# One core, a recurrent attention with a two-layer MLP behind it: the u row on ScalarE's DMA queue, and a new order of all operations

## The chip, the cores and the metric

The kernel runs on one core of a Trainium2 chip. A core has five engines with an instruction stream each: TensorE (PE in the profile; its weight loads are listed apart as PEld), VectorE (DVE), ScalarE (ACT), GpSimd (POOL) and SyncE (SP). Each of them takes its instructions in program order, and waits on semaphores that the others raise. DMA transfers are issued by an engine's instruction stream and run beside the engines.

The metric is the device time of one launch in microseconds, less is better. The kernel before takes 183.4 us, the median of three runs (182.93 to 184.22). "Within 1%" below means within 1.8 us.

## The reference, cut to what matters

Batch B = 4, heads H = 8, sequence S = 768, head dimension D = 48; the attention's output is the MLP's input, with 3072 tokens, 384 channels and 2048 hidden units.

```python
for t in range(S):
    cur = np.einsum('bhd,bhe->bhde', u[None] * kt, vt)
    y[:, :, t] = np.einsum('bhd,bhde->bhe', rt, state + cur)
    state = wt[:, :, :, None] * state + np.einsum('bhd,bhe->bhde', kt, vt)
...
h = x @ w_in
r = np.maximum(h, 0.0)
g = s * (r * r) + b
return (g @ w_out).astype(np.float32)
```

`u` is one row of 8 x 48 numbers. It enters only through `sum_d r*k*u` of the same step, a scalar for each token and head, which multiplies v.

## The kernel before, in words

The sequence is cut into 24 chunks of 128 tokens (6 for each of 4 batches), numbered n = 0 to 23. Two chunks make one tile T of 256 tokens for the MLP, so T = 0 to 11. Chunks 0 to 3 are "packed": two of them are loaded and decayed together (`load2`, L316; `load`, L308, for the others).

The steps of a chunk have short names, which the order uses. `load n.0` to `n.3` fetch w, r, k and v. `ln` takes the logarithm of w on ScalarE, `cum` sums it over the tokens with a triangular matmul (L390, L397, L408), `exp` (L438) and, from chunk 8, `inc` and `exn` give the decays. `mul` (L465, L472, VectorE) multiplies r and k by them, `tr` (L521) transposes the products on TensorE and `tev` copies them out of PSUM; from chunk 9 a transposing DMA replaces both. `mt` (L588, L600) forms the 128 x 128 scores, `msk` (L612, VectorE, four for a pair of chunks) masks them, `ymm` (L637, L650, L659) multiplies them by v (cast by `vb`). `rkp` and `rku` (L344, L350, GpSimd) form r*k and r*k*u, `cd` (L367, VectorE) sums over d, and `yd` (L373, GpSimd) multiplies v by it. `dmm`, `sup` (L759, L767) and `st` (L776) carry the state. `yev` brings the output to SBUF: for a packed chunk by the helper `move`, which takes ScalarE or VectorE as the order says; for the others by one VectorE instruction that also adds `yd` (L741). `xtr` (L787) transposes it, `xev` copies it into the tile's input.

The MLP of a tile is eight steps `g1 T.i` (six matmuls each, L841; step i needs the weight piece that its columns lie in: pieces 0 and 1 for i = 0 and 1, piece 2 for i = 2 and 3, and so on), each followed by `relu T.i` (L854) and `sq T.i` (L864 on ScalarE, L866 on VectorE), and eight steps `g2 T.i` (four matmuls each, L884), with `oev` (L895) and `store` at the end. The weights arrive in five pieces: `li` loads and `ci` casts a piece of w_in, `lo` and `co` one of w_out (L809, L821, casts at L964, L966, L968). `csred`, `csadd`, `cssplit`, `csspread` and `csevac` sum w_out over its rows for the bias b (L925, L932, L935, L943, L949).

The order of all of this is written out by hand as one text, `ORDER`. A program walks it word by word and emits each operation's instructions at once, so each engine's stream is the text's order, cut down to that engine. `name@A`, `@D` or `@P` sets the field `eng` of the operation to ScalarE, VectorE or GpSimd; `+6` puts in six matmuls on zeros (L1263) that keep TensorE occupied. Whether a mark has an effect is up to the operation's function: `move` and `cast` read the field, `square` and `csred` and `csadd` do. Two functions do not, that of `relu` and, for chunks 4 to 23, that of `yev`:

```python
        nc.scalar.activation(out=rh, in_=hs[T, i], func=AF.Relu)
...
        nc.vector.tensor_tensor(
            out=x,
            in0=c["y_ps"][:, 0:HD],
            in1=c["yd"].rearrange("t h d -> t (h d)"),
            op=ALU.add,
        )
```

All DMAs go out from SyncE, in the text's order. `load_u` (L983) is the second of them; `u_mm` (L987) then spreads the row over 128 partitions by a matmul with ones, and `u_ev` copies it to `u_bc`, which `rku` reads. Each DMA takes one of eight completion semaphores in turn, so a DMA can be issued only when the eighth before it has landed.

PSUM has six buffers "P" (cum, tr, mt, ymm, dmm, xtr, g1) and two "o" (g2, and the packed chunks' ymm); a buffer is given on in the text's order.

Of the kernel before, what the change touches and what calls it, by code (L numbers as in the profile page):

```python
# [18 lines left out]
U_AT = 3.5  # L19
# [23 lines left out]
load0.0 load_u load0.1 load0.2 ln0 +6 u_mm cum0.0 cum1.0 cum1.1 exp0.0 exp0.1 load2.0 li0 load2.1  # L43
exp1.0 u_ev@A l20 l21 load0.3 rkp1 rku1 load2.2 mul0.0 mul0.1 +4 tr0 exp1.1 mul1.0 ln2 +4 cum2.0
rkp0 mul1.1 tr1 tev0@D exp2.0 cum3.0 cd1 tev1@A vb0@A exp2.1 vb1@A +3 mt0 rku0 li1 cum3.1 ci0@A rkp3
exp3.0 rkp2 mul2.0 load2.3 msk1.0 exp3.1 ci1@A li3 li2 msk0.0 lo0 msk1.1 +3 ymm0.0 msk0.1 cd0 dmm0
ymm0.1 mul2.1 sup0 yd0 yd1 vb3@A vb2@A rku3 st0 mul3.0 l23 sup1 load4.0 tr2 ymi0 ydm0 lo1 rku2
mul3.1 tr3 tev2@A yev0@A xtr0 yev1@D xtr1 xev0@D ci3@P cd3 tev3@A xev1@A ci2@A mt2 cd2 g10.0 msk2.0
yd2 g10.1 l22 yd3 relu0.0 co0@A li4 msk3.0 msk2.1 co1@P g10.2 ymm2.0 lo2 ln4 lo3 load5.0 dmm2 msk3.1
sup2 ymm2.1 st2 g10.3 csred0@D ydm2 cum4.0 sq0.0@A relu0.2 ci4@P relu0.1 ymi2 yev2@D g10.4 sq0.2@A  # L50
relu0.3 xtr2 sup3 csred1@D exp4.0 sq0.1@D small2 g10.5 co2@D g10.6 xev2@A lo4 yev3@A xtr3 csadd1@D
sq0.3@A relu0.4 csred2@D relu0.6 load4.1 g10.7 relu0.5 g20.4 xev3@A sq0.4@A co3@D ln5 csadd2@D
sq0.5@A g20.0 cum4.1 g20.5 g20.1 g11.0 g11.1 load4.3 load7.0 csred3@D relu0.7 co4@D sq0.6@A csadd3@D
cum5.0 g11.2 sq0.7@A load5.1 load4.2 l24 csred4@D small cum5.1 g20.6 load5.2 relu1.1 relu1.0 g20.2
relu1.2 exp4.1 csadd4@D cssplit sq1.0@A load5.3 g20.3 g11.3 mul4 g11.4 vb5@P exp5.0 g11.5 exp5.1
sq1.1@A sq1.2@A vb4@A relu1.3 relu1.4 rkp4 rkp5 g20.7 csspread g11.6 tr4 load8.0 load6.0 csevac mul5
rku4 l25 oev0.1 relu1.5 tev4@A tr5 tev5@D oev0.0 rku5 dmm4 load7.3 load6.1 sup4 load6.2 relu1.6
g11.7 g21.0 mt4 msk4.0 msk5.0 load6.3 load7.1 sq1.3@A sq1.4@A sq1.5@A sq1.6@A relu1.7 st1 g21.1
g21.4 g21.5 dmm5 ln6 load9.0 msk4.1 cd4 yd4 ymm4 cum6.1 msk5.1 cum6.0 ln7 cd5 sup5 ln8 st4 exp6.0
cum7.0 g21.2 sq1.7@A exp6.1 vb6@A g21.6 cum7.1 yev4 exp7.0 vb7@P st5 ymm5 g21.3 xtr4 exp7.1 cum8.0  # L60
yd5 l26 ln9 mul6 tr6 yev5 xev4@D st3 load7.2 exp8.0 xtr5 dmm6 mul7 cum9.0 g21.7 tr7 tev6@A inc8
xev5@A sup6 load10.0 load11.0 l28 dmm7 load8.3 load8.1 load11.3 load9.1 l27 sup7 exp9.0 g12.0 g12.1
tev7@A relu2.0 inc9 oev1.0 rkp6 mt6 rku6 rkp7 relu2.1 store0.0 load8.2 msk6.0 sq2.1@A g12.2 ln10
sq2.0@A g12.3 st7 cd6 exn9 exn8 relu2.3 relu2.2 sq2.3@A load9.2 store0.1 msk6.1 oev1.1 g12.4 msk7.0
sq2.2@A rku7 st6 yd6 msk7.1 g22.0 ymm6 g22.4 load9.3 g12.5 cd7 yev6 relu2.4 ymm7 g12.6 yd7 vb8@P
xtr6 cum10.0 g12.7 rkp9 l29 mul8 ln11 relu2.5 exp10.0 rkp8 relu2.6 xev6@D load10.1 yev7 g22.1 inc10
# [24 lines left out]
load18.2 store4.1 store4.0 rku17 g16.7 rku16 sq6.3@A sq6.2@A sq6.5@A load20.0 yev15 sq6.4@D load21.1
xtr14 cum19.0 dmm16 g26.0 load21.0 load19.1 xtr15 g26.1 xev14@D relu6.6 g26.2 xev15@D sup16 relu6.7
sq6.7@A exp19.0 g17.0 g17.1 cd17 relu7.0 load20.1 inc19 cd16 sq7.0@A vb17@P yd16 vb18@A load19.2
mt16 msk16.0 msk16.1 g26.5 sq6.6@A g17.2 msk17.0 st16 relu7.1 g26.6 dmm17 sup17 msk17.1 g17.3 ymm16
g26.7 yev16 oev6.1 rkp18 relu7.2 relu7.3 ymm17 g17.4 load20.2 yd17 st17 g26.3 xtr16 oev6.0 sq7.1@A
exn18 xev16@D yev17 g17.5 g17.6 load21.2 load19.3 ln20 exn19 rku18 mul18 g27.4 xtr17 sq7.2@A relu7.4
g27.0 g17.7 sq7.4@A relu7.5 relu7.6 ln21 sq7.5@D store5.0 xev17@D cum20.0 sq7.3@A rkp19 relu7.7 cd18
g18.0 mul19 l219 g18.1 vb19@P rku19 exp20.0 sq7.6@A load22.0 inc20 sq7.7@D cum21.0 g18.2 g27.5 g27.1
g27.6 exn20 relu8.0 tev18 g18.3 relu8.1 relu8.2 exp21.0 g27.2 dmm19 store5.1 sq8.2@A g27.3 g27.7
mul20 inc21 exn21 dmm18 relu8.3 sq8.0@D tev19 sq8.1@A cd19 mul21 g18.4 load23.0 g18.5 yd19 rkp20  # L100
g18.6 sup18 tev21 sup19 oev7.1 oev7.0 relu8.4 ln22 yd18 rkp21 mt18 sq8.3@A relu8.5 g28.0 st18
msk19.0 supn21 msk18.0 msk19.1 tev20 msk18.1 load20.3 rku20 g28.4 g18.7 load22.1 store6.1 relu8.6
# [66 lines left out]
def kernel(  # L169
# [812 lines left out]
    def load_u():  # L982
        nc.sync.dma_start(out=u_row, in_=u.rearrange("h d -> (h d)").unsqueeze(0))  # L983
# [320 lines left out]
```

## Time and profile before

| What | Value | How to read it |
|---|---|---|
| Median of 3 runs | 183.4 us | 182.93 to 184.22 |
| Profiled execution, first to last instruction | 180.1 us | the only time that the page gives for it; 3.3 us less than the median, which lie around the span |
| TensorE clock granted | 1.00 in every stage | no throttling in this run |
| matmuls `g1` (L841) | 576, 72.2 us busy | 0.65 us for a step of six, back to back |
| matmuls `g2` (L884) | 400, 72.3 us busy | 0.65 us for a step of four, back to back |
| zero matmuls (L1263) | 20, 7.2 us busy | all before 15 us |
| relu (L854, ScalarE) | 96, 597 ns each | 54.5 us busy |
| square on ScalarE / VectorE | 77 of 635 ns / 19 of 534 ns | L864, L866 |
| DMA queues | one, 34.22 MB | 82.0% of 16 engines' span |

Busy time is counted once where instructions of an engine overlap in part. Four masks in a row take 2.48 us where one alone takes 0.68.

### The profile page before, as it was taken

How to read it: one execution, taken by the hardware profiler on the slowest of the kernel's cores; microseconds unless marked ns; L12 is line 12 of the kernel's file. 1: busy time of each engine (PE TensorE's matmuls, PEld its weight loads, DVE VectorE, ACT ScalarE, POOL GpSimd, SP SyncE). 2: the span in 40 equal slices, each digit the busy share in tenths (PEclk: the TensorE clock that was granted, in tenths of full speed). 3: DMA queues.
4: the chain of work that ended last, by engine and by line, in shares of the span. 5: the costliest groups of instructions: out<-in, count | busy, mean ns of one | idle time of the engine just before them, and what ended most of it. 6: DMA issues, size and time to landing. Idle time of an engine off the chain costs nothing.

```text
span 180.1 us, 4874 instructions
## 1 busy us (share of the span) xinstructions
PE 172.5 (96%) x1880; PEld 132.4 (74%) x1880; DVE 139.4 (77%) x251; ACT 143.4 (80%) x281; POOL 105.2 (58%) x141
## 2 busy tenths in 40 slices
PE   6997789999999999999999999999999999999993
PEld 2364568787688877888876879688777796796872
DVE  7499879998989899688699789678779795750341
ACT  2668799999999999798989769679968869266850
POOL 3687963009988987990689269484388382620000
PEclk9999999999999999999999999999999999999999
DMA  5999999999898969979988976999949845622022
GB/s 136 319 275 280 384 398 349 233 190 220 173 228 195 194 133 185 206 180 240 189 192 158 241 159 131 226 216 210 192 93 220 195 108 118 186 73 67 0 87 87
DMA packets 115722, 34.53 MB, mean 192 GB/s; under 512 B 110065, under 2 KB 113906, under 8 KB 115698
## 3 DMA queue, kind: packets, MB, share of 16 engines
q1 hardware_dynamic: 115698, 34.22, 82.0%
q8 instruction: 14, 0.23, 0.5%
q14 instruction: 10, 0.08, 0.2%
HBM read 25.17 MB, written 4.72 MB: 166 GB/s over the span
## 4 chain that ended last, share of the span: by engine, by line
PE 85%; SPq 7%; DMA 5%; ACT 1%; issue 0%; DVE 0%
PE o_ps L884 35%; PE h_ps L841 35%; DMA wi_st<-in_moe_w_in_dram 5%; SPq L316 5%; PE mt_ps L600 3%; PE cums L408 2%; PE y_ps L659 2%; SPq L809 2%; PE y_ps L650 2%; PE xt_ps L787 2%; PE d_ps L724 2%; PE trps L521 1%; ACT w_in L964 1%; PE cums L414 1%; PE yp_ps L637 0%
## 5 line engine op out<-in xcount | busy, mean ns | idle before, releaser
L841 PE MATMUL h_ps<-xT,w_in 128*128 128x256 bf16 x576 | 72.2, 273 | 0.6 <-ACT w_in L964 0.6
L884 PE MATMUL o_ps<-w_out,gT 128*128 128x384 bf16 (+2 forms) x400 | 72.3, 320 | 0.0
L854 ACT ACTIVATE rh<-h_ps 128x512 bf16<-128x512 f32 x96 | 54.5, 597 | 17.3 <-PE h_ps L841 16.8
L841 PEld LDWEIGHTS <-w_in 128*128 128x128 bf16 x576 | 60.0, 110 | 6.4 <-ACT w_in L964 0.9
L884 PEld LDWEIGHTS <-gT 128*128 128x128 bf16 x400 | 36.0, 98 | 18.0
L864 ACT ACTIVATE gT<-rh 128x512 bf16<-128x512 bf16 x77 | 47.0, 635 | 0.4
L612 DVE TENSOR_TENSOR mt_sb<-mt_ps,tri_strict 128x512 bf16<-128x512 f32 x40 | 25.5, 684 | 6.0 <-PE mt_ps L600 5.8
L350 POOL TENSOR_TENSOR rku<-rkp,u_bc 128x384 f32<-128x384 f32 x24 | 25.9, 1081 | 0.7 <-DVE cd L367 0.2
L373 POOL TENSOR_TENSOR yd<-vt,cd 128x384 bf16<-128x384 f32 x20 | 17.9, 896 | 13.6 <-DMA vt<-in_v_dram 6.4
L344 POOL TENSOR_TENSOR rkp<-rkt 128x384 f32<-128x384 f32 x20 | 20.1, 1008 | 4.7 <-DMA rkt<-in_k_dram 4.7
L472 DVE TENSOR_TENSOR prd<-rkt,E 128x768 bf16<-128x768 f32 x20 | 21.9, 1101 | 0.2 <-ACT E L438 0.2
L438 ACT ACTIVATE E<-cums 128x388 f32<-128x388 f32 (+2 forms) x32 | 15.3, 495 | 5.5 <-POOL rku L350 1.7
L895 DVE SCALAR_TENSOR_TENSOR o_sb<-o_ps,s_bc,bconst 128x384 f32<-128x384 f32 (+2 forms) x25 | 14.8, 596 | 5.8 <-PE o_ps L884 5.7
L966 POOL CAST vb<-vt 128x384 bf16<-128x384 f32 x11 | 7.5, 679 | 16.4 <-DMA vt<-in_v_dram 16.4
L866 DVE TENSOR_TENSOR gT<-rh 128x512 bf16<-128x512 bf16 x19 | 10.0, 534 | 7.5 <-ACT rh L854 7.5
L776 POOL TENSOR_TENSOR st<-stmp,l 128x384 bf16<-128x384 bf16 x16 | 14.7, 918 | 0.4 <-DVE stmp L767 0.4
L508 POOL TENSOR_TENSOR l<-E,par 128x8 f32<-128x8 f32 x20 | 6.9, 353 | 11.8 <-ACT E L438 11.7
L741 DVE TENSOR_TENSOR x_sb<-y_ps,yd 128x384 bf16<-128x384 f32 x20 | 10.7, 552 | 4.0 <-PE y_ps L659 4.0
L367 DVE TENSOR_REDUCE cd<-rku 128x8 f32<-128x384 f32 x24 | 13.0, 543 | 0.3 <-POOL rku L350 0.3
L767 DVE TENSOR_TENSOR stmp<-d_ps,st 128x384 bf16<-128x384 f32 x16 | 8.6, 551 | 2.2 <-PE d_ps L724 1.7
L465 DVE TENSOR_TENSOR prd<-pkt,E 128x384 bf16<-128x384 f32 x8 | 7.0, 892 | 2.3 <-ACT E L438 2.2
L446 DVE TENSOR_TENSOR inc<-cums,logw_two 128x384 f32<-128x384 f32 x11 | 6.1, 551 | 3.0 <-PE cums L414 1.7
(103 smaller groups left out, 205.4 us busy)
## 6 DMA issues: line engine op xcount, KB each, us to landing
wt<-in_w_dram SPq DMA_DIRECT2D x20, 192.0 KB, 4.0
rkt<-in_r_dram SPq DMA_DIRECT2D x20, 192.0 KB, 3.7
vt<-in_v_dram SPq DMA_DIRECT2D x20, 192.0 KB, 3.5
rkt<-in_k_dram SPq DMA_DIRECT2D x20, 192.0 KB, 3.8
out_dram<-o_sb SPq DMA_DIRECT2D x19, 192.0 KB, 2.8
wi_st<-in_moe_w_in_dram SPq DMA_DIRECT2D x3, 768.0 KB, 8.1
wo_st<-in_moe_w_out_dram SPq DMA_DIRECT2D x3, 768.0 KB, 5.9
pkt<-in_w_dram SPq DMA_DIRECT2D x2, 384.0 KB, 4.4
```

The source lines that it names most:

```text
L344: nc.gpsimd.tensor_tensor(out=rkp, in0=c["r"], in1=c["k"], op=ALU.mult)
L350: nc.gpsimd.tensor_tensor(out=rku.rearrange("t h d -> t (h d)"), in0=c["rkp"].rearrange("t h d -> t (h d)"), in1=u_bc, op=ALU.mult,)
L373: nc.gpsimd.tensor_tensor(out=yd, in0=c["v"], in1=c["cd"].unsqueeze(2).to_broadcast([128, H, D]), op=ALU.mult,)
L438: nc.scalar.activation(out=c["E"][:, x, 0:w], in_=ps[:, 0:w], func=AF.Exp, scale=-1.0 if packed(n) and x else 1.0,)
L472: nc.vector.tensor_tensor(out=prd[:, :, :, 0:D], in0=c["rk"], in1=c["E"][:, :, 0:HD].rearrange("t x (h d) -> t x h d", h=H), op=ALU.mult,)
L612: nc.vector.tensor_tensor(out=c["mt"][:, sg], in0=c["mt_ps"][sg], in1=(masks[:, n % 2] if packed(n) else tri_strict) .unsqueeze(1) .to_bro ...
L776: nc.gpsimd.tensor_tensor(out=c["st_new"], in0=c["stmp"].rearrange("q p (g e) -> q p g e", g=2), in1=c["l2"].unsqueeze(3).to_broadcast([12 ...
L841: nc.tensor.matmul(ps[:, f, :], lhsT=w_in_sb[PIECE[ft]][:, kt, :].rearrange("p (m j) -> p j m", j=PIECES[PIECE[ft]])[:, ft - F0[PIECE[ft]] ...
L854: nc.scalar.activation(out=rh, in_=hs[T, i], func=AF.Relu)
L864: nc.scalar.activation(out=g, in_=rh, func=AF.Square)
L884: nc.tensor.matmul(os_[T, k][:, cols], lhsT=gT[T][:, ft, tt * 128 : (tt + 1) * 128], rhs=w_out_sb[PIECE[ft]][:, ft - F0[PIECE[ft]], cols], ...
L895: nc.vector.scalar_tensor_tensor(out=o_sb[:, cols], in0=os_.pop((T, k))[:, cols], scalar=s_bc, in1=bconst[:, cols], op0=ALU.mult, op1=ALU.add,
```

## The change

The row u is loaded by a DMA that ScalarE issues as its first instruction, ahead of the load of its activation table; `load_u` is gone from SyncE's stream and from the plan. The order text is new from beginning to end. The numbers of zero matmuls go from 6, 4, 4, 3, 3 to 4, 2, 2, 2, 4, at other places. Nothing else in the code differs.

```diff
-U_AT = 3.5
...
 ORDER = """
-load0.0 load_u load0.1 load0.2 ln0 +6 u_mm cum0.0 cum1.0 cum1.1 exp0.0 exp0.1 load2.0 li0 load2.1
-exp1.0 u_ev@A l20 l21 load0.3 rkp1 rku1 load2.2 mul0.0 mul0.1 +4 tr0 exp1.1 mul1.0 ln2 +4 cum2.0
-rkp0 mul1.1 tr1 tev0@D exp2.0 cum3.0 cd1 tev1@A vb0@A exp2.1 vb1@A +3 mt0 rku0 li1 cum3.1 ci0@A rkp3
-exp3.0 rkp2 mul2.0 load2.3 msk1.0 exp3.1 ci1@A li3 li2 msk0.0 lo0 msk1.1 +3 ymm0.0 msk0.1 cd0 dmm0
...
++4 load0.0 u_mm load0.2 load0.1 rkp0 ln0 +2 cum0.0 load2.0 load2.2 cum1.0 load0.3 exp0.0 u_ev@D
+exp0.1 rkp1 exp1.0 cum1.1 rku0 rku1 l21 exp1.1 mul0.0 l20 mul0.1 mul1.0 ln2 mul1.1 +2 tr0 tev0@A +2
+tr1 vb1@A tev1@D cum2.0 li2 exp2.0 load2.1 vb0@P cum3.0 cd0 exp3.0 exp2.1 cd1 mt0 ci2@A msk0.0
+msk1.0 +4 dmm0 msk1.1 ymm0.0 li0 msk0.1 load2.3 cum3.1 yd0 sup0 li1 small2 ymm0.1 mul2.0 st0 yd1
+ydm0 mul2.1 exp3.1 rkp2 mul3.0 yev0@A mul3.1 small sup1 ymi0 yev1@A xtr0 tr2 xtr1 ci0@A rkp3 li3
+rku2 li4 tr3 rku3 xev0@A lo0 tev2@A xev1@D vb3@P g10.0 ci1@A tev3@D load4.0 cd2 relu0.0@A l22 cd3
+mt2 lo1 msk2.0 load5.0 g10.1 yd2 vb2@A msk3.0 g10.2 relu0.1@A sq0.0@A msk2.1 yd3 msk3.1 g10.3 ymm2.0
+ci3@P relu0.3@A lo3 dmm2 ymm2.1 ydm2 sup2 lo2 st2 ymi2 sq0.3@A l23 yev2@D relu0.2@A g10.4 ci4@P xtr2
...
+    u_row = work.tile([128, HD], FP32, name="u_row", tag="inc", bufs=2)[0:1]
+    nc.scalar.dma_start(out=u_row, in_=u.rearrange("h d -> (h d)").unsqueeze(0))
     nc.scalar.preload_act_table_set("natural_log_exp_and_others")
...
-    u_row = work.tile([128, HD], FP32, name="u_row", tag="inc", bufs=2)[0:1]
...
-    def load_u():
-        nc.sync.dma_start(out=u_row, in_=u.rearrange("h d -> (h d)").unsqueeze(0))
...
-    add("load_u", "SP", 0.5, load_u, (), [], [], U_AT, dma=0.1)
-    add("u_mm", "PE", 0.85, spread_u, (), ["load_u"], [("o", ["u_ev"])], 2.0, lat=0.2)
+    add("u_mm", "PE", 0.85, spread_u, (), [], [("o", ["u_ev"])], 2.0, lat=0.2)
```

Counted over the whole text, these marks differ:

| Operation | before | after |
|---|---|---|
| sq on ScalarE / VectorE | 77 / 19 | 63 / 33 |
| relu marked @A / @D | none marked | 75 / 21 |
| yev of chunks 4 to 23 marked @A / @D | none marked | 16 / 4 |
| vb on ScalarE / VectorE / GpSimd | 13 / 0 / 11 | 10 / 3 / 11 |
| tev on ScalarE / VectorE | 6 / 3 | 4 / 5 |
| xev on ScalarE / VectorE | 10 / 10 | 11 / 9 |
| co of pieces 0, 1, 3 | ScalarE, GpSimd, VectorE | VectorE, VectorE, GpSimd |
| csred of piece 3; csadd of pieces 2 and 3 | VectorE | GpSimd |
| u_ev | ScalarE | VectorE |

## The prediction

> **What bounds the kernel now.** I read the page's slices first, then the busy time by stage, then the chain that ended last, then what TensorE waited for.
>
> ```profile
> span 180.1 us, 4874 instructions
> PE 172.5 (96%) x1880; PEld 132.4 (74%) x1880; DVE 139.4 (77%) x251; ACT 143.4 (80%) x281; POOL 105.2 (58%) x141
> PE   6997789999999999999999999999999999999993
> DVE  7499879998989899688699789678779795750341
> ```
>
> The cuts of the stages below are the starts of g1 0.0 (21.59), 1.0, 2.0, 3.0 and 4.0 and the end of the last matmul (177.20). Columns: stretch, its length, then busy us of each engine.
>
> ```profile
> 0.00:21.59 21.59, 17.54 (x208) 9.08 (x209) 17.09 (x40) 13.66 (x23) 15.35 (x33) 1.00 0.94 275
> 21.59:32.65 11.06, 10.48 (x139) 8.14 (x133) 9.79 (x17) 10.52 (x21) 5.63 (x7) 1.00 1.06 368
> 32.65:51.86 19.21, 19.21 (x216) 14.99 (x214) 17.93 (x30) 18.80 (x40) 11.00 (x16) 1.00 1.03 200
> 51.86:62.62 10.76, 10.76 (x134) 9.14 (x133) 10.01 (x18) 10.69 (x22) 10.29 (x13) 1.00 0.97 201
> 62.62:77.13 14.51, 14.51 (x158) 11.37 (x157) 12.33 (x22) 12.95 (x28) 12.69 (x16) 1.00 0.90 179
> 77.13:177.20 100.07, 100.02 (x1041) 79.71 (x1038) 71.99 (x128) 76.73 (x153) 50.26 (x60) 1.00 0.73 157
> 177.20:180.10 2.90, 0.00 (x0) 0.00 (x0) 0.31 (x1) 0.00 (x0) 0.00 (x0) 1.00 0.21 68
> ```
>
> From 32.65 to 177.20 TensorE is idle for 0.05 us in all: after the start it is the bound, and nothing that only moves work among the others can gain there. Before it, the chain of waits (start, us, what) names the gate, and TensorE's waits after 23.7 us are one line:
>
> ```profile
> 13.34 8.77 DMA wi_st<-in_moe_w_in_dram
> ...
> 22.13 1.48 ACT w_in L964
> ...
> 23.65 0.85 PE h_ps L841 x6
> ```
>
> ```profile
> PE h_ps L841 <- ACT w_in L964: 0.6, 1, 0.6
> ```
>
> The third w_in piece lands at 22.1, is cast until 23.6, and holds g1 0.2. So the time is the start of g1 0.0, plus TensorE's work from there (155.0 us busy from 21.59 to 177.20), plus its stalls (0.6), plus a tail of 2.9. I price the change in these four terms.
>
> **The start.** The new order asks for piece 2 as the seventh load, before the packed r and v and pieces 0 and 1. Landings are taken from this trace by volume: loads of 384 KB landed at 4.4, 6.0, 7.1, 8.4, 10.4, 11.6, 12.8 and 14.0, the tenth at 16.8, the twelfth at 20.3, the fourteenth at 22.1 (768 KB counted as two). In the new order v of chunks 0 and 1 lands at 11.6, piece 2 at 14.0, r of chunks 2 and 3 at 15.4, piece 0 at 16.8, piece 1 at 20.3, piece 3 at 22.1, piece 4 at about 24. No g1 of tile 0 waits for a load any more if the casts follow at once: piece 2 is cast (1.47) by 15.6, piece 0 (0.84) by 18.3, piece 1 by 21.1, pieces 3 and 4 on GpSimd (1.46 each) by 24.4 and 26.0.
>
> What is late next is chunk 1's output, through VectorE:
>
> ```profile
> 7.40 3.75 DVE L465 TENSOR_TENSOR prd<-pkt,E 128x384 bf16<-128x384 f32 x4 [2.22 <-ACT E L438]
> 13.78 2.48 DVE L612 TENSOR_TENSOR mt_sb<-mt_ps,masks 128x512 bf16<-128x512 f32 x4 [0.28 <-PE mt_ps L588]
> ```
>
> The first four products end at 11.15 as before. The second transpose (0.61) ends at 11.8, its copy on VectorE (0.68) at 12.6, where ScalarE's ended at 13.05; mt (0.64) ends at 13.4. Two cd (0.47 each in a row) run meanwhile, four masks (2.48) end at 16.0, sup at 16.4, four products at 0.7 each at 19.2, sup of chunk 1 (0.55) at 19.75, its xev (0.35) at 20.1. g1 0.0 starts at 20.1 to 20.2 and not at 21.59. On the way yd is done at 14.9, where the old order had TensorE wait for it until 19.0 (L677). After g1 0.0 come mt of the second pair (0.55), g1 0.1 at 21.4, g1 0.2 and 0.3, and every input of g1 0.4 to 0.6 is ready ahead of its turn by the casts above. I take 20.2. Its bounds: 19.6 if GpSimd disturbs the later products less (548 ns was the shortest of the eight, 1354 the longest), 21.6 if one more landing or one product is as slow as the slowest.
>
> **The load of u.** One DMA issue (0.46 on SyncE, at 1.26) leaves SyncE's stream, so k0 and everything behind it go out 0.46 earlier; ScalarE gets an issue ahead of its table load (1.28), which then ends at about 2.5, while its next instruction waits for w until 4.5: nothing. Who waits for u is u_mm, and behind it on TensorE the first cum. It waited 0.35 for u, until 4.28, and the first cum needs 5.8. Four zero matmuls of 0.43 instead of six end at 2.9. If u lands at 4.3 again, u_mm (1.61) and two zero matmuls (0.86) end at 6.8, 1.0 late; if it lands at once, nothing is late or gained, since the logarithm of w ends at 5.36. I take 0.1, nearest to the row in which u stood behind a 384 KB load and landed within 3.0 us: that is in the 20.2.
>
> The Trainium skill ("DMA: Bandwidth & Descriptors", section "Issuing engines are not separate DMA queues") says that DMAs of all engines run on the same 16 DMA engines, and that another issuer only saves sequencer time. That would leave just the 0.46; no run here shows the second queue yet.
>
> **Zero matmuls.** 20 become 14, all in time in which TensorE waits for others; their 7.2 us are no part of the 155.0. If the clock stayed lower for lack of them, cum, tr and mt on the path (some 2.5 us of matmuls) could take up to that much longer; the granted clock was 1.00 throughout, so I take 0.
>
> **TensorE's work after g1 0.0** grows by the mt that is now behind it: 155.0 + 0.5 = 155.5.
>
> **The middle.** From g1 0.0 to g1 4.0 VectorE was busy 9.79 + 17.93 + 10.01 + 12.33 = 50.1 of 55.5 us. Between the same two marks the new order gives it 93 operations for 77: four cd (2.2), two tev (1.4), eight squares (4.3 at 534 ns), one each of sup, inc, xev and vb (1.9), two half casts of w_out (1.0, half the row of 951 ns each), less one full cast, one csred and two csadd (3.5): 7.2 more, so 57.3 us against 56.0 for TensorE. VectorE, not TensorE, would then set the pace there, by 1.3 us if it never idles. Operations in a row overlap by 0.06 to 0.08, which takes off a little, and a few waits add; I take a stall of 1.2. Below: 0, since TensorE stood still for neither VectorE nor ScalarE in this stretch though ScalarE was 98% busy from 32.65 to 62.62. Above: 4.6, as under the rivals.
>
> A price in this sum rides on GpSimd, which was idle from 28 to 40 us and now gets a cast, a csred and two csadd there (1.46, some 3.0 by its 1.0 per 384 columns, 2.0):
>
> ```profile
> L866 DVE TENSOR_TENSOR gT<-rh x19: 410/425/1210, 28.5 to 172.8; 128x512 bf16<-128x512 bf16 x19
> L472 DVE TENSOR_TENSOR prd<-rkt,E x20: 939/952/1758, 38.8 to 147.3; 128x768 bf16<-128x768 f32 x20
> ```
>
> The same square took 410 or 1210 ns, the same product 939 or 1758; the square of 1210 ran at 85.6 beside an rkp on GpSimd. The skill ("GPSIMD Engine Reference", section 8, "Key points") names a cause: GpSimd shares its SBUF interfaces with VectorE, and VectorE's instructions with two SBUF inputs contend. Were all eight added squares stretched so, they would cost 9.7 and not 4.3, and the stall would be 6.6.
>
> **After g1 4.0** VectorE had 28 us idle in 100, and ScalarE loses seven squares there, six of which go to it (3.2 us); I add 0.
>
> **Sum:** 20.2 + 155.5 + 1.2 + 2.9 = 179.8, against 180.1 of the profiled execution: 0.3 less, so 183.1 for a median of 183.4.
>
> **Rivals.** *VectorE keeps up.* For it: TensorE never waited in 150 us. Against: 57.3 of 56.0. With a start at 19.6 to 20.0 and no stall the span is 178.0 to 178.4, the time 181.3 to 181.7; only the lower part is faster by over 1%.
>
> *VectorE becomes the bound of tiles 0 to 3, with its waits* (slower). It waits for matmuls and GpSimd's results; from 32.65 to 77.13 these waits were 3.3 us (0.8 for y, 0.8 for E, 0.4 for rkp, the rest smaller). If they stay on top of 57.3, the stall is 57.3 + 3.3 - 56.0 = 4.6: span 183.2, time 186.5. It decides from a stall of 3.3 on (185.2). Against it: a late VectorE finds its inputs ready, so waits shrink.
>
> *The change doesn't do what it says.* The 21 relus marked for VectorE still run on ScalarE, the 16 yev marked for ScalarE on VectorE, as no function reads these marks. ScalarE's sum is harmless (143.4, less 14 squares of 0.635 and some copies), but each such operation stands in a stream in which the order expected none, and everything behind it is up to 0.6 us late. The bounds are 0, by TensorE's waits above, and 21 x 0.6 + 16 x 0.55 = 21 if each reached TensorE. I take 0 into the forecast, nearest to the row; if one in six reaches it, 3.5 are added: 186.6.
>
> **Chances.** A change under 1% (1.8 us) is no more than a measurement of this kernel tells from none. Forecast, within 1%: 0.47, about 183.1. VectorE keeps up and the start is early, faster: 0.20. VectorE the bound: 0.19. Unread marks: 0.14. So faster 0.20, same 0.47, slower 0.33. The range goes from 181.2, the early start without stalls, to 186.5, the second rival; what lies beyond (the marks at more than 3.4, a still earlier start) I give 0.2.
>
> **What would show it.** Right: g1 0.0 between 19.6 and 20.8, no wait of TensorE for a w_in cast, piece 2 landed by 15; VectorE over 95% busy between g1 0.0 and 4.0, and TensorE's waits there for VectorE (products, outputs, masks) of about 1.2 us. Wrong: a first cum after 6.8 (u late); g1 0.0 after 21; waits of TensorE behind 77 us for squares or outputs (the marks); or TensorE without waits from 24 us on, with all of the early start kept.

## The result: slower by 9.5 %, and the profile after

| | before | after |
|---|---|---|
| median (range), us | 183.44 (182.93 to 184.22), 4 runs | 201.03 (200.62 to 201.53), 4 runs |
| ratio, with its 95 % interval | | 1.0947 [1.0906, 1.0989] |
| span of the profiled execution | 180.1 | 198.8 (of 200.62) |

The lines of the page of after that answer to the first fence of the prediction, and under them the granted clock:

```profile
span 198.8 us, 4886 instructions
PE 178.3 (90%) x1874; PEld 133.3 (67%) x1874; DVE 160.6 (81%) x266; ACT 133.2 (67%) x262; POOL 116.6 (59%) x145
PE   7776799892998969799999986899999999999994
DVE  7799848999999999999999998798699956423122
PEclk9999669998799999999999999999999999999999
```

VectorE did 15 more operations and was busy 21.2 us longer. Its row is all nines from the eighth slice to the 24th (35 to 119 us), and TensorE's has gaps that it did not have before. ScalarE lost 10 us of work and gained nothing by it. The clock, at full rate before, shows two dips.

The stages, cut at the starts of g1 0.0, 1.0, 2.0, 3.0 and 4.0 (columns as in the prediction):

```profile
21.90:32.92 11.02, 10.83 (x147) 8.32 (x148) 7.14 (x13) 6.76 (x14) 6.88 (x8) 0.73 0.91 279
32.92:62.17 29.25, 23.97 (x223) 16.63 (x221) 28.64 (x37) 18.79 (x38) 20.11 (x21) 0.94 0.93 187
62.17:75.46 13.29, 11.37 (x143) 9.53 (x141) 13.29 (x22) 9.93 (x20) 11.65 (x15) 1.00 0.47 102
75.46:91.83 16.37, 15.34 (x174) 11.82 (x172) 15.95 (x28) 11.25 (x24) 12.91 (x15) 1.00 0.97 189
```

The third engine figure, VectorE's, nearly fills the stage from 32.92 on (28.64 of 29.25 us, 13.29 of 13.29, 15.95 of 16.37). Over the four it is busy 65.0 us, where the prediction had 57.3. TensorE lost 14.0 us over the four, as worked out below. The chain by engine, before it 85 % PE:

```profile
PE 40%; DVE 25%; DMA 6%; issue 3%; SPq 2%; POOL 1%; DVEq 0%; POOLq 0%
```

And what TensorE waited for (total, times, longest):

```profile
PE trps L524 <- DVE prd L468: 4.1, 7, 0.9
PE csb_ps L946 <- DVE cs_sum L938: 2.7, 1, 2.7
PE xt_ps L790 <- DVE x_sb L744: 2.3, 2, 1.9
PE o_ps L887 <- DVE o_sb L898: 1.9, 3, 1.0
PE mt_ps L603 <- DMA RK<-prd: 1.5, 1, 1.5
```

(prd are the products of `mul`, RK these transposed; csb_ps belongs to csspread, xt_ps to `xtr`, o_ps to g2.) All but the last are VectorE's; the first lies before g1 0.0. To place the loss I take the start of each tile's g1 and subtract TensorE's work that the text puts ahead of it, which differs by up to 3 us between the two texts. TensorE is then 0.3 us late at g1 0.0, 3.3 at g1 1.0, 10.9 at 2.0, 13.0 at 3.0, 14.3 at 4.0, 15.7 at 6.0, 18.7 at 7.0 and 18.7 at its end: three quarters of the loss are made in tiles 0 to 3, the rest in tiles 4 to 6, nothing later.

**Why VectorE was fuller than its instructions say** is seen in its timeline (start, us, what), here the w_out block:

```profile
32.99 3.44 DVE L971 CAST w_out<-wo_st 128x768 bf16<-128x768 f32 x2
...
38.43 0.95 DVE L971 CAST w_out<-wo_st 128x1536 bf16<-128x1536 f32 x1
...
41.98 3.02 DVE L928 TENSOR_TENSOR wo_st<-wo_st 128x768 f32<-128x768 f32 x2
45.11 1.16 DVE L935 TENSOR_TENSOR wo_st<-wo_st 128x384 f32<-128x384 f32 x1
```

and GpSimd's beside it:

```profile
32.87 3.15 POOL L928 TENSOR_TENSOR wo_st<-wo_st 128x768 f32<-128x768 f32 x2
41.16 1.59 POOL L935 TENSOR_TENSOR wo_st<-wo_st 128x384 f32<-128x384 f32 x1 [5.15 <-ACT rh L857]
...
43.59 1.00 POOL L935 TENSOR_TENSOR wo_st<-wo_st 128x384 f32<-128x384 f32 x1
```

Two half casts took 3.44 us while GpSimd added, where a whole one, of the same size as both, took 0.95 at 38.43 with GpSimd idle. In the kernel before the same block ran on VectorE from 25.7 to 38.8, while GpSimd stood idle from 28.6 to 40.1, waiting for v. From the timeline of before:

```profile
35.77 1.55 DVE L925 TENSOR_TENSOR wo_st<-wo_st 128x768 f32<-128x768 f32 x2
...
40.12 0.88 POOL L966 CAST vb<-vt 128x384 bf16<-128x384 f32 x1 [11.48 <-DMA vt<-in_v_dram]
```

The same two sums took 3.02 us in after. Not every meeting costs VectorE: a whole cast at 40.94 in after kept its 0.95 us, and GpSimd's addition, which began 0.22 us behind it, took 1.59 us where the next took 1.00. Sorted over the whole trace, by whether GpSimd was busy for under 5 % or over 60 % of the operation (mean us, count):

| VectorE operation, inputs | before, clear | before, beside | after, clear | after, beside |
|---|---|---|---|---|
| gT, square (two in SBUF) | 0.42 (9) | 0.81 (5) | 0.42 (12) | 0.82 (19) |
| prd of chunks 4 to 23 (two in SBUF) | 0.95 (5) | 1.22 (11) | 0.95 (5) | 1.44 (14) |
| prd of chunks 0 to 3 (two in SBUF) | (0) | 0.89 (8) | (0) | 1.20 (8) |
| mt_sb (PSUM and SBUF) | 0.68 (3) | 0.68 (34) | 0.68 (8) | 0.68 (29) |
| x_sb (PSUM and SBUF) | 0.55 (4) | 0.55 (14) | 0.55 (7) | 0.55 (12) |
| cd, a reduction (one in SBUF) | 0.54 (8) | 0.54 (14) | 0.54 (9) | 0.54 (14) |

What reads PSUM, and the reduction, does not change by 0.01 us. Of what reads two operands from SBUF the square doubles, and a product takes 1.22 or 1.44 us for 0.95. Call stretch what an operation takes over the tenth percentile of its form (shapes and types) in all traces together. Summed over VectorE's operations between g1 0.0 and g1 6.0 it is 3.8 us before and 18.4 after (3.5 and 16.5 where each trace gives its own percentiles); the undisturbed work grew only from 75.6 to 80.8. ScalarE's, counted in the same way, is 2.5 and 1.9. The Trainium skill ("GPSIMD Engine Reference", section 8, "Key points") says that GpSimd shares its SBUF interfaces with VectorE and contends with instructions that have two SBUF inputs or run in a two-port mode. For two inputs the table agrees; whether a cast, with one, ran in such a mode no row here shows.

### The profile page after: what moved, and what is told of

Its sections match the earlier page's. It is cut to its first block, busy times and chain, and to the rows that moved or that the text cites. A ratio compares the mean times of both kernels' runs of the same rounds, so it can differ in the third digit from the quotient of the medians.

```text
span 198.8 us, 4886 instructions
## 1 busy us (share of the span) xinstructions
PE 178.3 (90%) x1874; PEld 133.3 (67%) x1874; DVE 160.6 (81%) x266; ACT 133.2 (67%) x262; POOL 116.6 (59%) x145
## 4 chain that ended last, share of the span: by engine, by line
PE 40%; DVE 25%; DMA 6%; issue 3%; SPq 2%; POOL 1%; DVEq 0%; POOLq 0%
PE o_ps L887 19%; PE h_ps L844 15%; DVE prd L475 4%; DMA rkt<-in_k_dram 4%; DVE mt_sb L615 4%; DVE gT L869 3%; DVE o_sb L898 2%; DVE x_sb L744 2%; DVE inc L449 2%; DVE stmp L770 2%; DVE cd L370 2%; DMA rkt<-in_r_dram 2%; DVE wo_st L928 2%; PE mt_ps L603 1%; SPq L920 1%
## 5 line engine op out<-in xcount | busy, mean ns | idle before, releaser
L844 PE MATMUL h_ps<-xT,w_in 128*128 128x256 bf16 x576 | 75.3, 279 | 0.4 <-DVE stmp L770 0.2
L867 ACT ACTIVATE gT<-rh 128x512 bf16<-128x512 bf16 x63 | 38.2, 635 | 0.3
L353 POOL TENSOR_TENSOR rku<-rkp,u_bc 128x384 f32<-128x384 f32 x24 | 28.6, 1194 | 3.6 <-DVE cd L370 3.0
L376 POOL TENSOR_TENSOR yd<-vt,cd 128x384 bf16<-128x384 f32 x20 | 18.4, 924 | 18.5 <-DVE cd L370 17.0
L475 DVE TENSOR_TENSOR prd<-rkt,E 128x768 bf16<-128x768 f32 x20 | 26.1, 1312 | 2.0 <-ACT vb L967 2.0
L869 DVE TENSOR_TENSOR gT<-rh 128x512 bf16<-128x512 bf16 x33 | 21.4, 658 | 6.5 <-ACT rh L857 6.5
L347 POOL TENSOR_TENSOR rkp<-rkt 128x384 f32<-128x384 f32 x20 | 22.3, 1116 | 4.3 <-DVE stmp L770 4.0
L370 DVE TENSOR_REDUCE cd<-rku 128x8 f32<-128x384 f32 x24 | 12.8, 541 | 0.0
L524 PE MATMUL trps<-shift,prd 128*128 128x128 bf16 x72 | 6.7, 235 | 4.8 <-DVE prd L468 4.1
L459 ACT ACTIVATE E<-inc 128x384 f32<-128x384 f32 x16 | 8.4, 537 | 3.2 <-DVE inc L449 3.2
L468 DVE TENSOR_TENSOR prd<-pkt,E 128x384 bf16<-128x384 f32 x8 | 9.1, 1200 | 1.4 <-ACT E L441 1.4
L524 PEld LDWEIGHTS <-prd 128*128 128x128 bf16 x72 | 4.6, 104 | 7.4 <-DVE prd L468 5.9
```

What stands on the lines that cost most here:

```text
L347: nc.gpsimd.tensor_tensor(out=rkp, in0=c["r"], in1=c["k"], op=ALU.mult)
L353: nc.gpsimd.tensor_tensor(out=rku.rearrange("t h d -> t (h d)"), in0=c["rkp"].rearrange("t h d -> t (h d)"), in1=u_bc, op=ALU.mult,)
L370: nc.vector.reduce_sum(out=cd, in_=c["rku"], axis=AX.X)
L376: nc.gpsimd.tensor_tensor(out=yd, in0=c["v"], in1=c["cd"].unsqueeze(2).to_broadcast([128, H, D]), op=ALU.mult,)
L475: nc.vector.tensor_tensor(out=prd[:, :, :, 0:D], in0=c["rk"], in1=c["E"][:, :, 0:HD].rearrange("t x (h d) -> t x h d", h=H), op=ALU.mult,)
L844: nc.tensor.matmul(ps[:, f, :], lhsT=w_in_sb[PIECE[ft]][:, kt, :].rearrange("p (m j) -> p j m", j=PIECES[PIECE[ft]])[:, ft - F0[PIECE[ft]] ...
```

## The experiments

Eighteen kernels ran. Times are medians (range) in us. Kernels with the new order spread by up to 4 us between runs (sq_act: 196.07 to 200.43), so a gain under 2 that rests on one profile is not called shown. The starts of the tiles, from the profiles, for kernels that share the new order of TensorE:

| kernel | g1 0.0 | g1 2.0 | g1 4.0 | g1 7.0 | last matmul ends |
|---|---|---|---|---|---|
| before (other order) | 21.6 | 51.7 | 77.0 | 114.7 | 177.2 |
| after | 21.9 | 62.2 | 91.8 | 133.1 | 195.9 |
| warm_both | 22.0 | 59.7 | 89.3 | 131.8 | 194.7 |
| cs_early | 21.9 | 60.0 | 90.5 | 132.9 | 195.7 |
| csum_dve | 22.0 | 58.4 | 88.9 | 128.8 | 191.6 |
| sq_act | 22.4 | 58.7 | 85.7 | 128.5 | 191.3 |
| loads_later | 21.9 | 61.8 | 91.4 | 132.1 | 194.9 |
| repaired | 22.0 | 57.8 | 85.5 | 126.8 | 189.6 |
| no_rk | 17.5 | 52.4 | 79.6 | 123.2 | 186.1 |
| no_rk_loads | 17.9 | 54.4 | 81.9 | 124.4 | 187.3 |

### Marks, order, or both

**relu_read.** The marks that no function reads, read:

```diff
-        nc.scalar.activation(out=rh, in_=hs[T, i], func=AF.Relu)
+        if pl.ops["relu", T, i]["eng"] == "DVE":
+            nc.vector.tensor_scalar_max(out=rh, in0=hs[T, i], scalar1=0.0)
+        else:
+            nc.scalar.activation(out=rh, in_=hs[T, i], func=AF.Relu)
```

> The 21 relus marked for VectorE run there. Theory 'VectorE and GpSimd hold each other up' (contention): VectorE is the engine that is full until 92 us, only one of the 21 relus lies before tile 3, so the time stays within 3 us of 201, and VectorE's busy time grows by some 12 us. Theory 'unread marks': the order gets what it was made for, and most of the 17.6 us goes: below 190.

201.51 (200.02 to 203.00), ratio 1.1004 [1.0793, 1.1215]. VectorE's busy time grew by 10.4 us to 171.0, and the 21 relus in its stream brought nothing: that half of the third rival of the prediction falls. The other half, the 16 yevs that are marked for ScalarE and run on VectorE, 0.55 us each (five of them ahead of g1 4.0 in the text), was not tried.

**order_new_marks_old** and **order_old_marks_new**: the order text of one kernel with the engine marks of the other.

> The new order with every engine mark set back to the old order's (relu and yev without marks). If the engine choice is the cause (contention through the four GpSimd sums and casts, and more squares on VectorE): below 188. If the sequence itself is the cause (which operations of VectorE and GpSimd meet, where TensorE waits): above 195. In between: both.

> The old order, u loaded by SyncE, with every engine mark of the new order. If the engine choice is the cause: above 192. If the sequence is: within 2 us of 183.4, or up to 187 for the added squares on VectorE.

201.71 (two runs, 199.35 and 204.08) and 198.50 (197.34 to 199.67; ratio 1.0840 [1.0667, 1.1012]). Each half alone costs nearly all of it, so the two costs do not add: 18 and 15 make 18. In the profile of order_new_marks_old VectorE is not full: it is busy 56.5 of the 67.1 us between g1 0.0 and 4.0, and its stretch to g1 6.0 is about 9. TensorE ends at 194.3 even so, 17 us later than before; its longest single wait, 4.4 us, is for a cast of w_out. So the new order is late also where VectorE is not the bound.

**old_sq_new.** One sort of mark alone, in the old order: a net 14 squares go to VectorE.

```diff
-... sq0.1@D ... sq0.4@A ... sq0.6@A ... sq1.0@A ... sq2.0@A ... sq11.6@D
+... sq0.1@A ... sq0.4@D ... sq0.6@D ... sq1.0@D ... sq2.0@D ... sq11.6@A
```

> One part alone: the kernel before with only the squares on the engines that the changed kernel marks (a net 14 go to VectorE). Theory contention: VectorE gets 14 x 0.42 = 5.9 us and as much again by stretch, of which 28 us of idle behind g1 4.0 hide all but the few in tiles 0 to 3: 185 to 189. If the marks cost only through the order they were made for: 193 to 198, as with all marks.

189.08 (187.90 to 189.52), ratio 1.0339 [1.0280, 1.0399]. Fourteen operations of 0.42 us on an engine that was "77 % busy" cost 5.9 us. It is hardly the contention that costs here: VectorE's stretch between g1 0.0 and 6.0 grew by 1.3 us. TensorE, which waited for no square before, now does:

```profile
PE o_ps L884 <- DVE gT L866: 1.7, 1, 1.7
```

What makes the rest of the 5.9 is not shown.

**hyb_before_after** and **hyb_after_before**: one text up to g1 2.0, then what is left of the other.

> The order and marks of before up to g1 2.0 (u on ScalarE's queue), then what is left in the order and with the marks of the changed kernel. If the loss is made in tiles 0 and 1 (10.9 us of it by the marks of the trace) and the rest of the new order only adds its own 8: g1 2.0 at 51.7 and 190 to 192. If the rest loses only because VectorE comes in late and full: 184 to 187. If the rest is bad by itself: 195 and over.

> The reverse: the changed kernel up to g1 2.0, then what is left in the order and with the marks of before. g1 2.0 at about 62 as in the changed kernel; if the rest of the old order keeps pace, 183.4 + 10.9 = 194 to 195; if the backlog of VectorE costs there too, 197 to 200.

195.88 (195.09 to 196.68; ratio 1.0674 [1.0545, 1.0802]) and 192.88 (ratio 1.0510 [1.0433, 1.0586]). After a good start (g1 2.0 at 53.2) the rest of the new text still loses 11 us; after a bad start (62.3) the rest of the old text loses nothing more (188.1 at the end of TensorE for 177.2, 10.9 late, as at g1 2.0). So the new text is slow in both parts, and the old one keeps pace even from behind.

### GpSimd beside VectorE

**no_rk**, and **no_rk_before** as its control:

```diff
-        nc.gpsimd.tensor_tensor(out=rkp, in0=c["r"], in1=c["k"], op=ALU.mult)
...
-        nc.gpsimd.tensor_tensor(
-            out=rku.rearrange("t h d -> t (h d)"),
...
-        nc.vector.reduce_sum(out=cd, in_=c["rku"], axis=AX.X)
+        nc.vector.reduce_sum(out=cd, in_=c.get("v", c["r"]), axis=AX.X)
```

> The changed kernel without GpSimd's two products per chunk, r*k and r*k*u (48 instructions); VectorE's reduction reads v in their place, so the diagonal term of the output is not the reference's. Order, marks and VectorE's instructions stay. Theory contention (VectorE's operations are stretched by 18.4 us between g1 0.0 and g1 6.0 beside GpSimd's, where the kernel before has 3.8): the stretch falls below 8, and TensorE, which VectorE holds up in tiles 0 to 6, ends 9 to 12 earlier: 189 to 192. Theory order (the sequence itself makes TensorE wait, whatever VectorE's operations last): 197 to 200.

> The control: the same 48 instructions left out of the kernel before (same edit). TensorE bounds it from 32.7 us on, so only the start can give: 182.4 to 183.4 under both theories. Below 181 the no_rk run would say nothing of the change alone.

Both leave out r*k and r*k*u, so their output is not the reference's. 191.75 (190.77 to 192.72; ratio 1.0448 [1.0301, 1.0596]): 9.3 us back, as the contention theory had it. The control: 184.05 (181.79 to 185.29; ratio 0.9983 [0.9930, 1.0035]), nothing. VectorE's groups of products, of after (busy, mean ns):

```profile
L475 DVE TENSOR_TENSOR prd<-rkt,E 128x768 bf16<-128x768 f32 x20 | 26.1, 1312 | 2.0 <-ACT vb L967 2.0
L468 DVE TENSOR_TENSOR prd<-pkt,E 128x384 bf16<-128x384 f32 x8 | 9.1, 1200 | 1.4 <-ACT E L441 1.4
```

and of no_rk:

```profile
L464 DVE TENSOR_TENSOR prd<-rkt,E 128x768 bf16<-128x768 f32 x20 | 20.8, 1042 | 4.6 <-ACT vb L956 3.7
L457 DVE TENSOR_TENSOR prd<-pkt,E 128x384 bf16<-128x384 f32 x8 | 4.0, 552 | 1.5 <-ACT E L430 1.4
```

The eight products of the start fell from 1200 to 552 ns, and with them g1 0.0 from 21.9 to 17.5: without the contention the new order does have its early start. Stretch between g1 0.0 and 6.0 fell from 18.4 to 9.4 (expected: under 8); over half of what is left is the w_out block, whose sums stayed on both engines. Two limits of this run. GpSimd's other work also comes earlier when 48 of its instructions go; but VectorE had not waited for rku in after (0.0 us idle before the 24 cd). And of the 9.8 us by which TensorE ends earlier 4.4 are won in the start, 2.5 between g1 0.0 and 1.0, 5.3 from there to g1 4.0, and 2.4 are lost again by g1 7.0; the 2.5 lie where after's clock is at half rate and no_rk's is not (see the clock below), so whether the products or the clock gave them is open.

**csum_dve.** The third w_out sum, two of the running sums and the fourth cast go back to VectorE:

```diff
-co3@P ... csred3@P ... csadd2@P ... csadd3@P
+co3@D ... csred3@D ... csadd2@D ... csadd3@D
```

> The changed kernel with four operations taken back from GpSimd to VectorE: cast and row sum of w_out piece 3 and the two additions. Contention: the two half casts fall from 3.44 to about 1.0 us, the row sum of piece 4 from 3.0 to 1.6, TensorE's 3.6 us wait for the bias sum shrinks to under 1.5, time 194 to 198 although VectorE does 3.5 us more. If VectorE is only overfull by its own work: 202 to 205. Unread marks: no change, 201.

198.88 (two runs, 196.80 and 200.96). In the profile of the 196.8 run the two half casts take 1.02 us with GpSimd idle, and TensorE waits 1.2 us for the bias sum instead of 3.6, as expected; the row sum of the last piece stays at 2.9. VectorE has 3.5 us more of its own work between g1 0.0 and 6.0 and 4.2 less stretch, and TensorE is 3.8 earlier at g1 2.0 and 4.3 at its end. But 2.7 of the 3.8 are there at g1 1.0, behind a stage in which this run's clock was at full rate and after's was not:

```profile
22.00:30.25 8.25, 8.06 (x148) 7.03 (x148) 6.98 (x15) 6.77 (x14) 5.43 (x6) 1.00 0.92 263
```

Against warm_both below, whose clock was up there too, csum_dve is 1.3 us earlier at g1 2.0 and 3.0 at the end. More work on the fullest engine, and no later end, points the same way as no_rk; two runs 4 us apart do not show it in the time.

**sq_act.** All 19 squares of tiles 0 to 6 that are marked for VectorE, on ScalarE:

```diff
-sq0.4@D ... sq0.6@D ... sq1.0@D ... sq6.7@D
+sq0.4@A ... sq0.6@A ... sq1.0@A ... sq6.7@A
```

> The changed kernel with the 19 squares of tiles 0 to 6 that it marks for VectorE on ScalarE, order unchanged. VectorE loses 19 x 0.42 = 8.0 us of work and the 5.8 to 7 that these were stretched by; ScalarE, which no trace shows stretched, gets 19 x 0.63 = 12.0 and has the room (67 % busy). Theory contention, VectorE the bound: 190 to 194. If ScalarE's stream then holds relu and the exponentials back as far: 199 to 202.

199.51 (196.07 to 200.43), ratio 1.0965 [1.0904, 1.1026]: not shown to be faster by this ratio. Three of the six runs took 196.07 to 198.91 and three 200.12 to 200.43, and the ratio fits the latter three; all six are below the four of after, so some gain is likely and its size is open. The profile is of the 196.07 run; there TensorE is 6.2 us earlier at g1 4.0 but only 3.3 at g1 6.0 (113.3 for 116.6). What is won in tiles 0 to 3 is partly lost in tiles 4 and 5. Here too 2.3 us of the lead are there at g1 1.0 (30.6 for 32.9), where the clock was up; against warm_both sq_act is 3.6 earlier at g1 4.0 and 3.3 at the end.

**cs_early** and **cs_early_warm.** The w_out block earlier in the order and on its old engines; in the second also zero matmuls (7 and 8).

```diff
-... relu0.1@A sq0.0@A ... ci4@P xtr2 ... xev3@D g10.6 ... sq0.4@D g11.1 co0@D ... co1@D sq0.6@D ...
-csred0@D csred1@D ... csadd1@D co2@D ... co3@P csred2@D ... csred3@P ... csadd2@P ... csadd3@P ... cssplit
+... relu0.1@A co0@A sq0.0@A ... msk3.1 csred0@D ... ci4@P co1@P xtr2 ... xev2@D csred1@D csadd1@D ...
+xev3@D co2@D csred2@D csadd2@D ... sq0.4@D co3@D csred3@D csadd3@D ... sq0.6@D co4@D csred4@D csadd4@D cssplit
```

> The changed kernel with the w_out casts, column sums and their split put earlier in the order and on the engines of before (first cast ScalarE, second GpSimd, the rest and all sums VectorE); all else as in the changed kernel. Theory VectorE's stream (the sums begin at 36.7 us, beside GpSimd's sums, and chunk 4's products wait behind them): csspread at about 41 to 43 and not 47.4, g1 2.0 at 54 to 56 and not 62.2, time 193 to 195. Theory clock: only the second dip goes, time 199 to 200. If the sequence elsewhere costs: no gain, over 200.

> Both edits (7 zero matmuls before g1 0.0 and 8 before csspread). If the two are all that was lost in front of 62 us: g1 2.0 at 51 to 53 as in the kernel before (51.7), time 189 to 191, the rest being lost behind 90 us. If they share one cause: no better than the better of the two alone, 193 to 196.

200.69 (198.75 to 200.97; ratio 1.0915 [1.0851, 1.0979]) and 201.36 (199.93 to 202.73; ratio 1.0999 [1.0922, 1.1076]): a miss. The sums ran earlier, but VectorE now reached the squares of tile 0 late: in the second's trace ScalarE's relu waits 3.0 us for one of them, and TensorE 2.1 us for the relu. Sorting did not help this full queue.

### The clock

**warm_both.** Zero matmuls in the waits before g1 0.0 (into its own PSUM tile) and before csspread:

```diff
+... +1 xtr0 +2 tr2 xtr1 +3 tr3 ... +1 g10.0 ...
+        for _ in range(12):
+            nc.tensor.matmul(ps, lhsT=warm_sb[:, 0:128], rhs=warm_sb[:, :d_model], start=True, stop=True)
```

> The changed kernel with 7 more zero matmuls in the waits before g1 0.0 (into g1 0.0's own PSUM tile) and 12 (384 wide) before csspread. Theory clock: the two half-clock stretches (21.1 to 27.9 and 48.4 to 51.8 us) cost TensorE 3.4 + 1.7 us and pass to the end: granted clock about 1.00, g1 1.0 at 29.5 and not 32.9, time 196. Theory VectorE's stream: it is full from 31 us on with the w_out sums, so the clock comes back but g1 2.0 stays within 1.5 us of 62.2 and the time is 199.5 to 201.

199.19 (198.96 to 202.87), ratio 1.0851 [1.0804, 1.0899]. The stage from g1 0.0 to 1.0, of warm_both, against the first line of the fence of after:

```profile
22.00:30.25 8.25, 8.06 (x147) 7.04 (x148) 6.99 (x15) 6.77 (x14) 5.98 (x7) 1.00 0.99 275
```

Granted clock 1.00 for 0.73, and 8.25 us for 11.02. So the first dip cost 2.7 us. The second (48.4 to 51.8 in after) cost nothing that is seen: from g1 1.0 to 2.0 TensorE takes 29.4 us without it for 29.3 with it, and VectorE is full in both. TensorE is 2.5 us earlier at g1 2.0, 4.0 and 6.0; half of that is lost from g1 6.0 to 7.0, where now warm_both's clock dips (120.5 to 123.9):

```profile
114.09:131.84 17.75, 15.60 (x158) 11.39 (x156) 13.98 (x22) 11.79 (x25) 9.66 (x12) 0.90 0.98 193
```

Left are 1.2 us at TensorE's end and some 1.8 in the median. Neither theory alone had this. That the zero matmuls held the clock up at 21 us is likely (the mean clock of the four runs is 0.97 to 1.00, that of after's four 0.96 to 0.97) but not shown: the dips move from execution to execution, and in the profiles of csum_dve and sq_act, without these matmuls, the clock did not fall there either.

**few_zero.** The kernel before with 4, 2, 2, 2, 4 zero matmuls for 6, 4, 4, 3, 3.

> The kernel before with 14 zero matmuls for its 20 (4, 2, 2, 2, 4 for 6, 4, 4, 3, 3), nothing else changed. Theory clock: it falls to half somewhere before 30 us and the time is 184.5 to 187. If it needs the longer waits of the new order before 21 us as well: clock 1.00 and 183.2 to 183.7.

182.88 (181.66 to 185.78), ratio 0.9974 [0.9938, 1.0009]: the number of zero matmuls costs nothing that can be measured, though the clock dips here too (21.5 to 24.9 us). So it does in the kernel before: of its 39 runs beside the experiments 23 had a mean granted clock of 0.98 to 0.99, at the same times (182.0 to 184.4, the others 181.6 to 184.2). The profile of before is of a run without a dip. That of few_zero:

```profile
PEclk9999879999999999999999999999999999999999
```

### SyncE's queue and the transfers

Two reasons in the trace of after spoke for transfers: the row 62.17:75.46 has a DMA share of 0.47, and TensorE waits for RK at 121. SyncE's stream there:

```profile
64.14 1.38 SPq L916 DMA_DIRECT2D out_dram<-o_sb  x2
73.31 1.35 SPq L561 DMA_TRANSPOSE RK<-prd  x1
```

The transpose waited 7.8 us for a product of VectorE, and with it every load behind it:

```profile
65.50:73.30 7.80, 6.33 (x82) 5.14 (x76) 7.80 (x12) 6.69 (x15) 6.39 (x7) 1.00 0.20 50
```

**sp_ahead.** Seven loads put ahead of that transpose:

```diff
-... store0.1 g13.2 ... tev9 ... load12.0 ... load14.1 ... load12.2
+... store0.1 load12.0 load14.1 load12.1 load14.2 load12.3 load14.3 load12.2 g13.2 ... tev9
```

> The changed kernel with seven loads of chunks 12 and 14, which stand behind the first RK transpose by DMA (chunk 9) on SyncE, put ahead of it. In the changed kernel that transpose waits 7.8 us (65.5 to 73.3) for a product of VectorE and SyncE's queue with it; the transfers' share is 0.20 there. Theory queue (the transfers lost there are missed at 104 to 133 us): share over 0.7 from 65 to 73, no wait for RK at 121, 196.5 to 198.5. Theory VectorE alone: the transfers go out, but TensorE is no earlier: 200 to 201.5.

200.11 (197.65 to 201.84), ratio 1.0846 [1.0743, 1.0949], which overlaps that of after. The same stretch with the loads ahead:

```profile
65.50:73.30 7.80, 5.87 (x73) 4.76 (x72) 7.80 (x11) 5.83 (x13) 7.20 (x9) 1.00 0.92 186
```

The transfers went out, VectorE was as full, and TensorE still waited for RK. In no_rk that transpose was issued at 62.4 without standing. The queue's standing is a mark of VectorE's lateness; a cost of its own is not shown.

**loads_later** and **no_rk_loads.** Eighteen loads of chunks 13 to 23, which the new text asks for earlier than the old one, moved 4 to 34 groups of matmuls back (`load23.1` from group 94 to 128, for one), with and without r*k.

> The changed kernel with those 18 loads put back, nothing left out. Theory transfers: 3 to 4 less, of the 3.0 lost between g1 6.0 and 7.0 and the waits before them, 197 to 198. Theory VectorE alone (transfers are late only where VectorE has let TensorE run ahead): 200 to 201.5.

> no_rk (r*k and r*k*u left out on GpSimd, v reduced instead) and also 18 loads of chunks 13 to 23, which the changed kernel asks for 4 to 34 groups of matmuls earlier than the kernel before, put back to where that kernel has them. no_rk kept 8.9 us of the loss, 6.9 of them between g1 4.0 and g1 7.0, where TensorE waited for RK and ScalarE and VectorE for w and v. Theory transfers (the loads pulled forward crowd out those that are needed next and the RK transposes): that stretch loses less than 2, time 185 to 188. Theory sequence of the rest: 190 to 192 as without it.

199.36 (197.80 to 200.72; ratio 1.0910 [1.0831, 1.0988]) and 191.81 (191.66 to 191.96; ratio 1.0499 [1.0424, 1.0574], no_rk having 1.0448): no gain shown. The theory that the loads pulled forward crowd out the next ones, which asked for 3 to 4 us, finds no support.

### All edits at once

**repaired.** The edits of sp_ahead, sq_act, csum_dve and warm_both (7 and 8 zero matmuls) together.

> All single edits in the changed kernel at once: the seven loads ahead, 19 squares of tiles 0 to 6 on ScalarE, the w_out sums (with the fourth cast) on VectorE, zero matmuls before g1 0.0 (7) and csspread (8). By the profiles they gave 4.6 (squares), 4.3 (sums) and 1.2 (zero matmuls) of the 18.7 us that TensorE's end is late. If they add, with 2 to 3 for the loads: 187 to 190. If they share one cause, VectorE's lateness in tiles 0 to 3: 193 to 196. If ScalarE becomes the bound in its place: over 196.

194.30 (193.09 to 194.63), ratio 1.0598 [1.0522, 1.0674]: 6.7 us back, the largest gain with all of the work done, and in the range expected for a shared cause. TensorE's end is 6.3 earlier. The single gains in the profiles (4.6, 4.3, 1.2 and none) make 10.1, but those three all start from a profile without the first clock dip. Taken against warm_both, so that this counts once, they are 3.3, 3.0 and 1.2, or 7.5: by these profiles the edits nearly add, and what they share is mostly the clock. No experiment gave a kernel that was shown to be faster than the one before.

## Why the prediction was wrong

The predicted span was 179.8, the measured 198.8. Of the 19.0 us, 1.7 lie in the start, 12.8 between g1 0.0 and 4.0, 4.4 between g1 4.0 and 7.0.

**The step that failed** is the price of VectorE's operations: "57.3 us against 56.0 for TensorE", bounded above by "4.6, as under the rivals". The added operations were counted rather high (7.2 us to g1 4.0; the undisturbed work grew by some 4 to there and by 5.2 to g1 6.0), but they, and those that were there already, were priced at durations from a trace in which GpSimd stood idle while VectorE summed w_out. The prediction named the cover ("GpSimd, which was idle from 28 to 40 us and now gets a cast, a csred and two csadd there") and even showed rows with 410 and 1210 ns for the same square, and then charged the stretch to the eight added squares alone, at most 6.6. It falls also on the products, the sums and some casts that meet GpSimd. Shown by the traces: 65.0 us busy for 57.3; of the 14.9 us more than before some 4 are work and some 12 stretch (neighbours overlap a little). Shown by no_rk: 9.3 us come back when GpSimd's products go, 2.5 of which may be the clock's. A smaller slip: the 56.0 for TensorE is the old length of the stretch plus the moved mt; by the busy rows it is 55.5.

**The second rival** (VectorE the bound) had the mechanism; its price, 4.6, was 14.0 between g1 0.0 and 4.0. It added the waits of before to a sum, where a full engine passes every delay on: into csspread (2.7), into ScalarE's relus, into SyncE's queue.

**The start**: landings right (the cast of piece 2 ran from 14.20 to 15.68 for a predicted 14.1 to 15.6, and g1 waited for no cast), but "the first four products end at 11.15 as before" did not hold. They took 5.01 for 3.75 us, the next four 4.12, beside rkp and rku, which the new text puts earlier. So g1 0.0 came at 21.90 for 20.2, above the stated 21.6, and at 17.5 in no_rk.

**u**: right that it is not late. It was there at 3.00, the first cum began at 5.41 for 5.82.

**Zero matmuls**: "the granted clock was 1.00 throughout, so I take 0" failed. It was 0.73 from g1 0.0 to 1.0; 2.7 us there, about 1.8 of the time (warm_both). That it comes of the smaller number is not shown: few_zero dips at no measured cost, and so do most runs of the kernel before. A clock of 1.00 in one trace tells nothing of the next run, or of a text with other gaps.

**After g1 4.0**: "VectorE had 28 us idle in 100", and so "I add 0", failed by 4.4. VectorE brought its backlog along and was full until 116:

```profile
91.83:116.56 24.73, 23.98 (x264) 19.24 (x261) 24.73 (x41) 20.36 (x43) 18.23 (x23) 1.00 1.00 211
116.56:133.08 16.52, 14.26 (x159) 10.66 (x156) 14.04 (x22) 11.69 (x25) 9.49 (x12) 1.00 1.13 201
```

**What stays open.** The stretch alone does not rank the kernels: order_new_marks_old, hyb_before_after, repaired and no_rk all have 8 to 10 us of it between g1 0.0 and 6.0, and TensorE ends 17, 13, 12 and 9 us later than before. Between g1 4.0 and 7.0 the new text needs 41.3 us; in no_rk, where VectorE is not full there, it needs 43.7, in repaired 41.3, for 36.9 of TensorE's work (the 41.3 less the 4.4 lost). The transfers' share is about 1.0 to 1.1, and TensorE waits for RK (4.2 us in no_rk). The two rows of no_rk there (g1 4.0 to 6.0, 6.0 to 7.0), VectorE idle for 3.5 and 5.0 us, the clock at half from 111.5 to 114.9:

```profile
79.56:105.28 25.72, 23.59 (x262) 19.20 (x261) 22.23 (x41) 20.36 (x43) 8.49 (x14) 1.00 1.02 206
105.28:123.24 17.96, 15.82 (x161) 11.42 (x159) 12.96 (x21) 11.73 (x25) 5.95 (x9) 0.90 1.05 200
```

Which transfer or which place in the order makes it was not found: neither moving 18 loads back nor putting seven ahead of the transpose was shown to change it. Of the 17.6 us by which the median rose, some 9 follow GpSimd's two products, and 8 to 9 are left without them, most of it in this stretch.

## What to carry to other kernels

Price an operation on VectorE twice, clear and beside GpSimd, before giving it work; if the sum with the dearer price passes the bound engine's time in any stage, expect VectorE to be the new bound, and expect each of its delays to reach the engines that wait for it. Look for what happened to be idle in the old trace: a duration is a property of its neighbours too. A square on ScalarE (635 ns, unstretched) takes less than one on VectorE beside GpSimd (0.82), though more than one in the clear (0.42). And before gains of single edits are read from profiles and added, look whether the clock dipped at the same places: here one dip that came or went was 2.7 us.

## What the runs showed of the hardware

VectorE's operations with two inputs in SBUF took 0.42 clear and 0.82 beside GpSimd (square), 0.95 and 1.44 (products); two half casts from 1.0 to 3.4 us; those that read PSUM did not change (0.68, 0.55). GpSimd pays less: rku had a mean of 1081 ns before and 1194 after.

TensorE's clock fell to half twice in after, from 21.1 to 27.9 and from 48.4 to 51.8 us. In the 3.4 us ahead of the first TensorE was busy for 1.55, ahead of the second, a wait of 3.6 us, for 0.34. In all traces the dips ahead of the last matmul are 3.4 or 6.8 us long, and traces of the same text up to that point have them at other places or not at all. The Trainium skill ("TensorE: Matmul & The Clock Gate", Part 1) says that the array's clock goes to half rate after at least one idle window of about 3.4 us; the lengths of the dips agree with that, but the window ahead of the first was not idle as a whole.
